# Output weights of two key heads in one transfer, mixed in pairs, in a decode attention kernel

## The chip, the cores and the metric

The kernel runs on one core of one Trainium2 chip. The metric is device time in microseconds (us) from launch to end, as the median of the executions in one set of rounds. Ratios below are the mean time of one kernel's fast runs over that of the kernel before's fast runs in the same rounds, so they are not quite the ratios of the medians quoted. A run counts as slow when it is over 1.5% above the fastest of its kernel; the medians and ranges below are of all runs, slow ones included. The profiled span is 1.7 to 3.1 us shorter than the time of the same execution. PE is TensorE, DVE is VectorE, ACT is ScalarE, SP is the engine that issues most DMAs. "Key tile 6" is the 4 MiB of keys of key head 6; heads are counted from 0.

## The reference, cut to what matters

```python
# B = 2, one query position, D = 448, 16 query heads on 8 key heads, Dh = 256, window W = 4096
q = (layernorm(x) @ wq)                       # 2 x 4096
p = softmax(q k^T / 16)                       # last 4096 cached keys of each key head
o = p v                                       # 2 x 16 x 256
out = x + o.reshape(2, 4096) @ wo + mish_mlp(layernorm(x))     # wo: 4096 x 448
```

The cached keys and values are 8 heads x (4 + 4) MiB. The output weights `wo` are 3.5 MiB, 512 rows of 896 bytes for each key head.

## The kernel before

Nearly everything streams through one DMA queue (77.66 of 77.81 MB), on which SP issues the loads. Per key head these are the next keys, the values, and the head's output weights:

```python
for i in range(Hkv + 1):
    if i + 1 < Hkv:
        load_k(i + 1, ...)
    if i < Hkv:
        load_v(i, ...)
        load_wo(i, parts=1 if i < Hkv - 1 else 2)
        for piece in range(NH):               # four pieces of a head's scores
            s = i * NH + piece
            if s + 1 < NSTEP: turn(s + 1)     # DVE transposes keys: kt <- k
            if piece == 1 and i > 1: finish(i - 2)
            scores(s)                         # PE: sc <- kt,qdiag, then exp on ACT
            ...
            if piece == 0 and i > 1: turn_o(i - 2)
            if piece == 1 and i > 1: mix(i - 2)
    ...
    if i >= 1: values(i - 1) or values_fixed(i - 1)   # the latter for heads 6 and 7
```

So the attention output of head i-2 is turned, scaled and multiplied with its weights ("mixed") inside head i. The heads 0 to 5 use this layout: partition p holds the four rows 4p to 4p+3 of the head's weights, one run of 3584 bytes, and mixing is four products over 128 partitions:

```python
wo_pool = tc.tile_pool(name="wo", bufs=3)
nc.sync.dma_start(out=w[:].rearrange("p h n -> p (h n)"),
    in_=A_wo[r0 : r0 + rep * Dh, :].rearrange("(p j) d -> p (j d)", p=P))   # load_wo
...
for j in range(NJ):                           # turn_o: NJ = 4, fp32, 8 rows x 128 columns
    for u in range(NP):                       # NP = 2
        nc.tensor.matmul(pqv[:, j, :], lhsT=o_sb[:, u, j, :, :]..., rhs=ident_f[...])
...
for j in range(NJ):                           # mix
    add(oT[:, j, :], w[...][:, j, :])         # psE += oT^T w, 2 x 448
```

In the trace of this kernel the 8 fp32 products of a turn leave 16 records a head (96 in the group of L516), the 4 bf16 products of a mix leave 4 (24 in that of L220).

After the last head, `mix(6)` (four products), a copy of the sum (`early`), `values_fixed(7)` and `mix(7)` follow one another on PE.

The softmax here doesn't subtract the row's maximum and nothing guards it: scores larger than these inputs give would overflow.

Of the kernel before, what the change touches and what calls it, by code (L numbers as in the profile page):

```python
# [9 lines left out]
ALU = mybir.AluOpType  # L10
AXIS = mybir.AxisListType
BF16 = mybir.dt.bfloat16
# [22 lines left out]
def kernel(  # L35
# [13 lines left out]
    nc = tc.nc  # L49
    P = 128  # L50
# [3 lines left out]
    Bsz, Sq, D = A_x.shape  # L54
    _, Hkv, Sk, Dh = A_k_cache.shape
    HqDh = A_wq.shape[1]
    Hq = HqDh // Dh
    rep = Hq // Hkv
    W = min(4096, max(256, Sk // 4))
    s0 = Sk - W  # L60
    F = B_w1.shape[1]
# [4 lines left out]
    BR = Bsz * rep  # L66
    NX = 2
    NS = D * NX // P
    HW = HqDh // NX
    HF = F // NX  # L70
    HH = Hq // NX
    NF = HF // P
    ND = Dh // P
# [8 lines left out]
    lead = ctx.enter_context(tc.tile_pool(name="lead", bufs=1))  # L82
    ident = lead.tile([P, P], BF16)
    hsel = lead.tile([P, Q], FP32)
    wo_pool = ctx.enter_context(tc.tile_pool(name="wo", bufs=3))
    k_pool = ctx.enter_context(tc.tile_pool(name="kk", bufs=2))
    v_pool = ctx.enter_context(tc.tile_pool(name="vv", bufs=2))
    kt_pool = ctx.enter_context(tc.tile_pool(name="kt", bufs=4))
    consts = ctx.enter_context(tc.tile_pool(name="consts", bufs=1))
    p_pool = ctx.enter_context(tc.tile_pool(name="pp", bufs=3))  # L90
    small = ctx.enter_context(tc.tile_pool(name="small", bufs=3))
# [6 lines left out]

    x_bf = consts.tile([Bsz, D], BF16)
    nc.scalar.dma_start(out=x_bf[:, :], in_=A_x.flatten_outer_dims())  # L100
    b1_sb = consts.tile([1, F], BF16)
    nc.scalar.dma_start(out=b1_sb[:, :], in_=B_b1.rearrange("(o f) -> o f", o=1))


    def v_tile():
# [7 lines left out]
    for lo, hi in ((0, SC), (SC, NS)):  # L113
# [16 lines left out]
        out=rstd[:], in_=mv[:, 1:2], func=ACT.Sqrt, bias=eps_t[:], scale=1.0  # L130
# [5 lines left out]
    for r in range(2):  # L136
        n = (NS + 1 - r) // 2
        nc.vector.tensor_scalar(  # L138
            out=xn_bf[:, r : NS : 2, :, :],
            in0=bass.AP(  # L140
                x_all.tensor,
                x_all.offset,
                [list(x_all.ap[0]), [1, n], [NS, P // 2], [(NS + r) // 2, 2]],
            ),
# [7 lines left out]
    for j in range(1, NQ):  # L152
        nc.vector.tensor_tensor(
            out=hsel, in0=hsel, in1=ident[:, j * Q : (j + 1) * Q : HS], op=ALU.add
# [4 lines left out]
    for b in range(Bsz):  # L159
        nc.vector.tensor_reduce(  # L160
            out=off[:, b : b + 1], in_=hsel[:, b * rep : (b + 1) * rep], axis=AXIS.X, op=ALU.add
# [4 lines left out]
        out=off[:], in0=off[:], scalar1=mine[:], scalar2=1e4, op0=ALU.subtract, op1=ALU.mult  # L166
    )

    PH = P // rep
    own = consts.tile([P, Bsz, rep], FP32)  # L170
    for h in range(rep):
        nc.vector.tensor_reduce(
            out=own[:, :, h],
            in_=ident[:, h * PH : (h + 1) * PH].unsqueeze(1).to_broadcast([P, Bsz, PH]),
            axis=AXIS.X,
            op=ALU.add,
        )
    ones_f = consts.tile([P, P], FP32)
# [10 lines left out]
    for s in range(NS):  # L189
# [7 lines left out]
        out=odd[:],  # L197
# [21 lines left out]
    def add(lhsT, w, start=False, stop=False):  # L219
        nc.tensor.matmul(  # L220
            psE[:], lhsT=lhsT, rhs=w, start=start, stop=stop, skip_group_check=True
        )
# [79 lines left out]
    def load_dense():  # L302
        w = v_tile()
        dense["w1"] = w[:, 0 : NS * HF].rearrange("p (s n) -> p s n", s=NS)
        nc.sync.dma_start(
            out=dense["w1"],
            in_=B_w1.rearrange("r (x n) -> (r x) n", x=NX).rearrange("(p s) n -> p s n", s=NS),
        )
        dense["w2"] = w[:, NS * HF : NS * HF + NX * NF * D].rearrange(
            "p (x c d) -> p x c d", x=NX, c=NF  # L310
        )
        nc.sync.dma_start(
            out=dense["w2"], in_=B_w2.rearrange("(x q c) d -> q x c d", x=NX, q=P)
        )

    def dense_in():
        w1_v = dense.pop("w1").rearrange("p s (q c) -> p s c q", c=NF)
        b1_v = b1_sb[:].rearrange("o (x q c) -> o x c q", x=NX, c=NF)
        hT_ps = ps_m.tile([P, NF, NX, Bsz], FP32, tag="m", name="hT_ps")
        for c in range(NF):  # L320
            for s in range(NS):
                nc.tensor.matmul(
                    hT_ps[:, c, :, :].rearrange("p x b -> p (x b)"),
                    lhsT=w1_v[:, s, c, :],
                    rhs=xs[:, s, :, :].rearrange("p x b -> p (x b)"),
                    start=(s == 0),
                    stop=False,
                    skip_group_check=True,
                )
            for x in range(NX):  # L330
                nc.tensor.matmul(
                    hT_ps[:, c, x, :],
                    lhsT=b1_v[:, x, c, :],
                    rhs=ones[:, :],
                    start=False,
                    stop=True,
                    skip_group_check=True,
                )
        shape = [P, NF, NX, Bsz]
        h_sb = consts.tile(shape, FP32, name="h_sb")  # L340
        nc.vector.tensor_copy(out=h_sb[:], in_=hT_ps[:])
        u_sb = consts.tile(shape, FP32, name="u_sb")
        nc.scalar.activation(out=u_sb[:], in_=h_sb[:], func=ACT.Exp)
        t_sb = consts.tile(shape, FP32, name="t_sb")
        nc.vector.scalar_tensor_tensor(
            out=t_sb[:], in0=u_sb[:], scalar=2.0, in1=u_sb[:], op0=ALU.add, op1=ALU.mult
        )
        den = consts.tile(shape, FP32, name="den_sb")
        nc.vector.tensor_scalar(
            out=den[:], in0=t_sb[:], scalar1=2.0, scalar2=None, op0=ALU.add  # L350
        )
        nc.vector.reciprocal(out=den[:], in_=den[:])
        nc.vector.tensor_tensor(out=t_sb[:], in0=t_sb[:], in1=den[:], op=ALU.mult)
        nc.vector.tensor_tensor(out=act_bf[:], in0=h_sb[:], in1=t_sb[:], op=ALU.mult)  # L354
# [27 lines left out]
        v_t[i] = t[:].rearrange("p (t d) -> p t d", t=T)  # L382

    def load_wo(kvh, parts=1):
        w = wo_pool.tile([P, rep, ND * D], BF16, tag="wo", name="wo")
        r0 = kvh * rep * Dh
        wo_t[kvh] = w
        if kvh < Hkv - NFIX:

            nc.sync.dma_start(  # L390
                out=w[:].rearrange("p h n -> p (h n)"),
                in_=A_wo[r0 : r0 + rep * Dh, :].rearrange("(p j) d -> p (j d)", p=P),
            )
            return
        win = A_wo[r0 : r0 + rep * Dh, :].rearrange("(h p c) d -> p h (c d)", h=rep, p=P)
        for u in range(parts):
            hs = slice(u * rep // parts, (u + 1) * rep // parts)
            nc.sync.dma_start(out=w[:, hs, :], in_=win[:, hs, :])  # L398
# [64 lines left out]
        return rec  # L463

    NJ = Dh // PH
    assert rep == 2 and NJ == rep * ND
    NP = 2
    NR = NP * BR

# [39 lines left out]
    def turn_o(i):  # L509

        o_sb = state.pop(("o", i))
        pq = ps_q.tile([P, NJ * BR], FP32, tag="q", name="q")
        pqv = pq[:].rearrange("p (j r) -> p j r", j=NJ)
        for j in range(NJ):
            for u in range(NP):
                nc.tensor.matmul(  # L516
                    pqv[:, j, :],
                    lhsT=o_sb[:, u, j, :, :].rearrange("r h m -> r (h m)"),
                    rhs=ident_f[0:NR, u * BR : (u + 1) * BR],
                    start=(u == 0 and j == 0),  # L520
                    stop=(u == NP - 1),
                    skip_group_check=True,
                )
        state["pq", i] = pqv

    def finish(i):
        pqv = state.pop(("pq", i))
        rec = state.pop(("rec", i))
        o = small.tile([P, NJ, Bsz, rep], FP32, tag="osum", name="osum")
        nc.vector.tensor_tensor(  # L530
            out=o[:].rearrange("p j b h -> p j (b h)"),
            in0=pqv,
            in1=rec[:].unsqueeze(1).to_broadcast([P, NJ, BR]),
            op=ALU.mult,
        )
        nc.vector.tensor_tensor(  # L536
            out=o[:].rearrange("p j b h -> p j (b h)"),
            in0=o[:].rearrange("p j b h -> p j (b h)"),
            in1=own[:].rearrange("p b h -> p (b h)").unsqueeze(1).to_broadcast([P, NJ, BR]),
            op=ALU.mult,  # L540
        )
        oT = small.tile([P, NJ, Bsz], BF16, tag="oTm", name="oTm")
        nc.vector.tensor_tensor(  # L543
            out=oT[:], in0=o[:, :, :, 0], in1=o[:, :, :, 1], op=ALU.add
        )
        state["oT", i] = oT

    def values_fixed(i):

# [16 lines left out]
        scale_o(i, po)  # L566

    def mix(kvh):
        oT = state.pop(("oT", kvh))
        w = wo_t.pop(kvh)  # L570
        put = add_last if kvh == Hkv - 1 else add
        if kvh < Hkv - NFIX:
            for j in range(NJ):
                add(oT[:, j, :], w[:].rearrange("p h (c d) -> p (h c) d", c=ND)[:, j, :])
            return
        for h in range(rep):
            for c in range(ND):
                put(
                    oT[:, c, h, :],
                    w[:, h, c * D : (c + 1) * D],  # L580
                    stop=(kvh >= Hkv - 2 and h == rep - 1 and c == ND - 1),
                )
# [80 lines left out]
```

## Time and profile before

| | before |
|---|---|
| median (first set of rounds) | 189.69 us, 6 runs, 189.51 to 193.02 (this last one slow) |
| profiled span | 187.9 us |
| DMA queue, share of 16 engines | 96.8% |
| PE, DVE, ACT busy | 81%, 57%, 24% |
| HBM read | 77.67 MB, 413 GB/s over the span |

The row to read first is the DMA share by slice: it is 8 or 9 tenths from the second slice to the last but one, so the bytes set the time as long as nothing behind the last byte is late. The lines of the page, the chain and the timeline that matter stand in the prediction.

### The profile page before, as it was taken

To read this page: it belongs to the slowest core of one execution; us is meant where nothing else is said; L and a number is where in the kernel's file an instruction comes from. 1 tells how busy PE (TensorE), PEld (TensorE's weight loads), DVE (VectorE), ACT (ScalarE), POOL (GpSimd) and SP (SyncE) were. 2 spreads that over 40 slices of the span, in tenths; PEclk is the share of its full clock that TensorE was granted. 3 is DMA by queue.
4 is the path that set the end of the run, shared out by engine and by line. 5 is a ranking of instruction groups with operands and counts; after the bars stand their busy time and mean duration, and the time that the engine had idled before them with its cause. 6 is when DMAs were issued, how large, how long until landed. Compare 5 with 4: busy or idle time off the path is not lost.

```text
span 187.9 us, 2493 instructions
## 1 busy us (share of the span) xinstructions
PE 151.5 (81%) x981; PEld 74.0 (39%) x981; DVE 106.9 (57%) x144; ACT 45.4 (24%) x148; POOL 16.5 (9%) x74
## 2 busy tenths in 40 slices
PE   0494099904989999979996999968995999999892
PEld 0141033901334364425342354434441534464781
DVE  5505497049671994089704991099506983976311
ACT  3005015200062225123322124033402223125101
POOL 7001500300003000200030003000110000000000
PEclk9999559965799999999999699999998799999955
DMA  6999899999999999999999999999999999999990
GB/s 224 420 474 446 376 434 439 439 443 446 433 446 419 406 407 436 446 439 393 472 445 440 412 426 412 440 446 418 451 433 439 394 436 419 443 439 415 412 381 27
DMA packets 5028, 77.81 MB, mean 414 GB/s; under 512 B 533, under 2 KB 1049, under 8 KB 2330
## 3 DMA queue, kind: packets, MB, share of 16 engines
q1 hardware_dynamic: 5012, 77.66, 96.8%
q8 instruction: 7, 0.11, 0.2%
q14 instruction: 3, 0.02, 0.0%
q10 hardware_dynamic: 6, 0.01, 0.0%
HBM read 77.67 MB, written 0.00 MB: 413 GB/s over the span
## 4 chain that ended last, share of the span: by engine, by line
DMA 67%; DVE 16%; PE 12%; SPq 2%; ACT 1%; issue 1%; ACTq 0%; DVEq 0%
DMA k<-in_A_k_cache_dram 57%; DVE kt L404 13%; DMA wo<-in_A_wo_dram 9%; PE sc L416 7%; PE o L477 4%; DVE pT L442 2%; SPq L373 1%; PE q L516 1%; ACT p L430 1%; PE psE L220 0%; SPq L114 0%; SPq L398 0%; PE psA L237 0%; DVE sums L451 0%; DVE osum L536 0%
## 5 line engine op out<-in xcount | busy, mean ns | idle before, releaser
L404 DVE STREAM_TRANSPOSE kt<-k 128x2048 f32<-128x2048 f32 x32 | 73.1, 2289 | 52.6 <-DMA k<-in_A_k_cache_dram 52.6
L416 PE MATMUL sc<-kt,qdiag 128*128 128x512 bf16 x256 | 65.2, 404 | 16.6 <-DVE kt L404 16.2
L430 ACT ACTIVATE p<-sc,off 128x256 bf16<-128x256 f32 x64 | 33.1, 544 | 70.9 <-PE sc L416 70.2
L416 PEld LDWEIGHTS <-qdiag 128*128 128x128 bf16 x256 | 23.8, 100 | 53.7 <-issue 23.5
L477 PE MATMUL o<-v,pT 128*8 128x512 bf16 x192 | 42.5, 379 | 0.0
L477 PEld LDWEIGHTS <-pT 128*8 128x8 bf16 x192 | 17.2, 92 | 22.4
L442 DVE STREAM_TRANSPOSE pT<-p 128x512 bf16<-128x512 bf16 x32 | 21.8, 681 | 5.8 <-ACT p L430 5.8
L289 POOL COPY qdiag<-qt 32x16 bf16<-32x16 bf16 x64 | 13.0, 249 | 120.0 <-PE sc L416 104.3
L486 ACT COPY o_sb<-o 8x512 f32<-8x512 f32 x12 | 6.3, 573 | 36.3 <-PE o L477 36.3
L516 PEld LDWEIGHTS q<-ident_f,o_sb 8*128 8x128 f32 x96 | 11.1, 186 | 3.1 <-issue 3.1
L430 ACT ACTIVATION_READ_ACCUMULATOR p<-sc,off 128x1 f32 x64 | 11.7, 183 | 0.0
L516 PE MATMUL q<-ident_f,o_sb 8*128 8x4 f32 x96 | 11.7, 249 | 0.0
L220 PE MATMUL psE<-v,act_bf 128*2 128x448 bf16 x14 | 4.9, 534 | 6.7 <-DVE act_bf L354 6.7
L269 PE MATMUL q_ps<-v,xq 128*128 128x512 bf16 x28 | 7.8, 446 | 2.5 <-DMA v<-in_A_wq_dram 2.5
L558 PEld LDWEIGHTS <-v 128*128 128x128 bf16 x256 | 7.4, 101 | 0.2 <-DMA v<-in_A_v_cache_dram 0.2
L558 PE MATMUL q<-pT,v 128*128 128x4 bf16 x256 | 7.4, 169 | 0.1
L220 PE MATMUL psE<-wo,oTm 128*2 128x448 bf16 x24 | 5.5, 352 | 1.4 <-DVE oTm L543 1.4
L269 PEld LDWEIGHTS <-xq 128*128 128x128 bf16 x28 | 3.1, 111 | 7.2 <-DVE xq L260 2.5
L279 DVE CAST q_sb<-q_ps 128x512 bf16<-128x512 f32 x2 | 1.3, 686 | 7.7 <-PE q_ps L269 7.7
L220 PEld LDWEIGHTS <-act_bf 128*2 128x2 bf16 x14 | 1.6, 117 | 9.7 <-DVE act_bf L354 6.8
L190 PE MATMUL xnT_ps<-ident,xn_bf 2*128 2x2 bf16 x7 | 0.5, 166 | 4.7 <-DVE xn_bf L138 4.7
L279 ACT CAST q_sb<-q_ps 128x512 bf16<-128x512 f32 x2 | 1.1, 589 | 12.0 <-PE q_ps L269 12.0
(62 smaller groups left out, 45.0 us busy)
## 6 DMA issues: line engine op xcount, KB each, us to landing
k<-in_A_k_cache_dram SPq DMA_DIRECT2D x7, 4096.0 KB, 27.3
v<-in_A_v_cache_dram SPq DMA_DIRECT2D x7, 4096.0 KB, 29.2
k<-in_A_k_cache_dram SPq DMA_DIRECT2D x2, 2048.0 KB, 24.6
v<-in_B_w_dram SPq DMA_DIRECT2D x2, 1568.0 KB, 24.5
wo<-in_A_wo_dram SPq DMA_DIRECT2D x7, 448.0 KB, 30.5
v<-in_A_wq_dram SPq DMA_DIRECT2D x1, 2048.0 KB, 7.4
v<-in_A_v_cache_dram SPq DMA_DIRECT2D x1, 2048.0 KB, 14.9
v<-in_A_wq_dram SPq DMA_DIRECT2D x1, 1536.0 KB
```

The lines of the kernel that those rows point to most:

```text
L220: nc.tensor.matmul(psE[:], lhsT=lhsT, rhs=w, start=start, stop=stop, skip_group_check=True)
L269: nc.tensor.matmul(ps[u][:], lhsT=xq[:, s, :, :].rearrange("p j k -> p (j k)"), rhs=wq_sb[:, s, u * N5 : (u + 1) * N5], start=(s == 0), st ...
L279: copy(out=q_sb[:, u * N5 : (u + 1) * N5], in_=ps[u][:])
L289: nc.gpsimd.tensor_copy(out=tv[rows, :, e, j * Q : (j + 1) * Q : HS].rearrange("p n (b h) -> p n b h", b=Bsz), in_=qv[rows, :, h0 : h0 + r ...
L404: nc.vector.transpose(out=kt[:].bitcast(FP32), in_=k[:, half * TH * Dh : (half + 1) * TH * Dh].bitcast(FP32),)
L416: nc.tensor.matmul(psc[:], lhsT=qdiag[i % NW][:, n * NE + e, :], rhs=ktv[:, n, e, :, :], start=(n == 0 and e == 0), stop=(n == NB - 1 and ...
L430: nc.scalar.activation(out=pv[:, b, :, :], in_=sv[:, b, :, :], func=ACT.Exp, scale=scale, bias=off[:, b : b + 1], accum_out=state["rs", i] ...
L442: nc.vector.transpose(out=pT[:], in_=p_t.pop(s)[:])
L477: nc.tensor.matmul(po[:], lhsT=pT_t[i * NH + piece][:, uh * NP * Q : (uh + 1) * NP * Q : HS], rhs=v[:, u * NP : (u + 1) * NP, :].rearrange ...
L486: nc.scalar.copy(out=o_sb[:, u, :, :, :], in_=po[:, u * Dh : (u + 1) * Dh] .rearrange("r (m j) -> r j m", j=NJ) .unsqueeze(2) .to_broadcas ...
L516: nc.tensor.matmul(pqv[:, j, :], lhsT=o_sb[:, u, j, :, :].rearrange("r h m -> r (h m)"), rhs=ident_f[0:NR, u * BR : (u + 1) * BR], start=( ...
L558: nc.tensor.matmul(po[:, c, :], lhsT=vv[:, t, c, :], rhs=pTv[:, th, 0:Q:HS], start=(t == 0 and c == 0), stop=(t == T - 1), skip_group_chec ...
```

## The change

The intent is longer runs and fewer transfers. Two key heads' weights (1024 rows) come in one transfer in which partition p holds eight rows, a run of 7168 bytes. The first head of a pair then lies on partitions 0 to 63 and the second on 64 to 127. The output of a head is turned with 64-column products onto its half of the partitions, and the pair is mixed together, eight products in the odd head. Two double buffers replace three single ones; the bias of the dense layer moves into the dense weights' tile to make room. Heads 6 and 7 keep their own layout.

```diff
-    wo_pool = ctx.enter_context(tc.tile_pool(name="wo", bufs=3))
+    wo_pool = ctx.enter_context(tc.tile_pool(name="wo", bufs=2))
...
-    PH = P // rep
+    NK = 2
+    PK = P // NK
+    PH = PK // rep
... (b1 load moved into the dense weights' tile; `own` mask rebuilt for two halves)
     def load_wo(kvh, parts=1):
+        if kvh < Hkv - NFIX:
+            if kvh % NK == 0:
+                w = wo_pool.tile([P, NJ * D], BF16, tag="wo", name="wo")
+                nc.sync.dma_start(
+                    out=w[:],
+                    in_=A_wo[r0 : r0 + NK * rep * Dh, :].rearrange("(p j) d -> p (j d)", p=P),
+                )
+                wo_t[kvh + NK - 1] = w
+            return
...
         pq = ps_q.tile([P, NJ * BR], FP32, tag="q", name="q")
+        k0 = i % NK * PK
+        pqv = pq[k0 : k0 + PK, :].rearrange("p (j r) -> p j r", j=NJ)
         for j in range(NJ):                      # NJ is now 8
             for u in range(NP):
                 nc.tensor.matmul(
...
+                    tile_position=(0, k0),
... (finish works on the head's half of the partitions)
     def mix(kvh):
+        if kvh not in wo_t:
+            return
...
-                add(oT[:, j, :], w[:].rearrange("p h (c d) -> p (h c) d", c=ND)[:, j, :])
+                add(oT[:, j, :], w[:, j * D : (j + 1) * D])
```

More of the change, by code (lines that the diff above doesn't have):

```diff
@@ L100 @@
     nc.scalar.dma_start(out=x_bf[:, :], in_=A_x.flatten_outer_dims())
-    b1_sb = consts.tile([1, F], BF16)
-    nc.scalar.dma_start(out=b1_sb[:, :], in_=B_b1.rearrange("(o f) -> o f", o=1))
     def v_tile():
@@ L173 @@
             out=own[:, :, h],
-            in_=ident[:, h * PH : (h + 1) * PH].unsqueeze(1).to_broadcast([P, Bsz, PH]),
-            axis=AXIS.X,
+            in_=ident[:].rearrange("p (k h m) -> p h k m", k=NK, h=rep)[:, h, :, :]
+            .unsqueeze(1)
+            .to_broadcast([P, Bsz, NK, PH]),
+            axis=AXIS.XY,
             op=ALU.add,
@@ L314, in load_dense @@
         )
+        lo = NS * HF + NX * NF * D
+        dense["b1"] = w[0:1, lo : lo + F]
+        nc.scalar.dma_start(out=dense["b1"], in_=B_b1.rearrange("(o f) -> o f", o=1))
     def dense_in():
         w1_v = dense.pop("w1").rearrange("p s (q c) -> p s c q", c=NF)
-        b1_v = b1_sb[:].rearrange("o (x q c) -> o x c q", x=NX, c=NF)
+        b1_v = dense.pop("b1").rearrange("o (x q c) -> o x c q", x=NX, c=NF)
         hT_ps = ps_m.tile([P, NF, NX, Bsz], FP32, tag="m", name="hT_ps")
@@ L384, in load_wo @@
     def load_wo(kvh, parts=1):
-        w = wo_pool.tile([P, rep, ND * D], BF16, tag="wo", name="wo")
         r0 = kvh * rep * Dh
-        wo_t[kvh] = w
-        if kvh < Hkv - NFIX:
-            nc.sync.dma_start(
-                out=w[:].rearrange("p h n -> p (h n)"),
-                in_=A_wo[r0 : r0 + rep * Dh, :].rearrange("(p j) d -> p (j d)", p=P),
-            )
-            return
+        if kvh < Hkv - NFIX:
[7 more added lines that the diff above has]
+            return
+        w = wo_pool.tile([P, NJ * D], BF16, tag="wo", name="wo")
+        w = w[:, 0 : rep * ND * D].rearrange("p (h n) -> p h n", h=rep)
+        wo_t[kvh] = w
         win = A_wo[r0 : r0 + rep * Dh, :].rearrange("(h p c) d -> p h (c d)", h=rep, p=P)
@@ L465 @@
     NJ = Dh // PH
-    assert rep == 2 and NJ == rep * ND
+    assert rep == 2 and (Hkv - NFIX) % NK == 0
     NP = 2
@@ L512, in turn_o @@
         pq = ps_q.tile([P, NJ * BR], FP32, tag="q", name="q")
-        pqv = pq[:].rearrange("p (j r) -> p j r", j=NJ)
+        k0 = i % NK * PK
+        pqv = pq[k0 : k0 + PK, :].rearrange("p (j r) -> p j r", j=NJ)
         for j in range(NJ):
@@ L528, in finish @@
         rec = state.pop(("rec", i))
+        rows = slice(i % NK * PK, (i % NK + 1) * PK)
         o = small.tile([P, NJ, Bsz, rep], FP32, tag="osum", name="osum")
+        ov = o[rows, :, :, :].rearrange("p j b h -> p j (b h)")
+        shape = [PK, NJ, BR]
         nc.vector.tensor_tensor(
-            out=o[:].rearrange("p j b h -> p j (b h)"),
-            in0=pqv,
-            in1=rec[:].unsqueeze(1).to_broadcast([P, NJ, BR]),
+            out=ov, in0=pqv, in1=rec[rows, :].unsqueeze(1).to_broadcast(shape), op=ALU.mult
+        )
+        nc.vector.tensor_tensor(
+            out=ov,
+            in0=ov,
+            in1=own[rows, :, :].rearrange("p b h -> p (b h)").unsqueeze(1).to_broadcast(shape),
             op=ALU.mult,
         )
+        if i % NK == 0:
+            state["oT", i + NK - 1] = small.tile([P, NJ, Bsz], BF16, tag="oTm", name="oTm")
         nc.vector.tensor_tensor(
-            out=o[:].rearrange("p j b h -> p j (b h)"),
-            in0=o[:].rearrange("p j b h -> p j (b h)"),
-            in1=own[:].rearrange("p b h -> p (b h)").unsqueeze(1).to_broadcast([P, NJ, BR]),
-            op=ALU.mult,
-        )
-        oT = small.tile([P, NJ, Bsz], BF16, tag="oTm", name="oTm")
-        nc.vector.tensor_tensor(
-            out=oT[:], in0=o[:, :, :, 0], in1=o[:, :, :, 1], op=ALU.add
-        )
-        state["oT", i] = oT
+            out=state["oT", i - i % NK + NK - 1][rows, :, :],
+            in0=o[rows, :, :, 0],
+            in1=o[rows, :, :, 1],
+            op=ALU.add,
+        )
     def values_fixed(i):
```

## The prediction

> **What bounds the kernel now.** I read the page first: the share of the DMA queues, then the row of slices.
>
> ```profile
> DMA  6999899999999999999999999999999999999990
> ...
> q1 hardware_dynamic: 5012, 77.66, 96.8%
> ```
>
> The one load queue keeps the 16 DMA engines busy for 96.8% of the span, and no slice but the first and the last is below 8 tenths. PE has 81% of the span busy and DVE 57%, so both should have spare time inside a head. Then the chain of waits in order of time, from the fifth key head on (start us, duration us, what):
>
> ```profile
> 112.92 29.40 DMA k<-in_A_k_cache_dram
> 142.31 0.02 issue
> 142.34 2.32 DVE kt L404
> 144.66 0.14 issue
> 144.80 3.44 PE sc L416 x8
> ...
> 156.51 7.02 PE o L477 x32
> ...
> 166.72 17.75 DMA wo<-in_A_wo_dram
> 184.47 0.04 issue
> 184.51 0.46 PE psA L237 x8
> ```
>
> It hops from one even key tile to the next (landings at 60.30, 101.30, 142.31, so 41.0 us for two heads), then goes through PE work, and ends in the landing of the last head's output weights. Two heads are 16 MiB of cache and 0.875 MiB of weights, 17.7 MB in 41.0 us or 431 GB/s: the stream sets the pace. What matters is whether the stream gets shorter, and whether anything at the tail stops fitting behind it. So third the timeline of PE at the end (start us, us, group, idle before it):
>
> ```profile
> 144.80 3.44 PE L416 MATMUL sc<-kt,qdiag 128*128 128x512 bf16 x8 [2.34 <-DVE kt L404]
> ...
> 165.30 1.94 PE L516 MATMUL q<-ident_f,o_sb 8*128 8x4 f32 x16
> 167.17 1.91 PE L416 MATMUL sc<-kt,qdiag 128*128 128x512 bf16 x8
> 169.02 0.92 PE L220 MATMUL psE<-wo,oTm 128*2 128x448 bf16 x4
> ...
> 179.87 3.96 PE L558 MATMUL q<-pT,v 128*128 128x4 bf16 x128
> 184.09 0.79 PE L237 MATMUL psA<-wo,oT 128*2 128x112 bf16 x16 [0.26 <-DVE oT L498]
> ```
>
> From the landing of key tile 6 PE works almost without a gap for 39 us, and it reaches the last output product at 184.09, only 0.4 us before the last weights land at 184.47. So there are two nearly equal paths to the end: the DMA stream, and "key tile 6 lands, then PE works through". Their margin is small: the wait for the last value piece (0.16 us in the timeline at 183.44) and the gap inside the last product (0.26 us at 184.52), together 0.42 us.
>
> [...]
> - [...] The trace agrees: in its packet records a 3584-byte packet takes 140 ns, 1792 bytes 74, 6272 bytes 239, 12544 bytes 469 and 32768 bytes 1213. The line through 1792 and 3584 leaves 8 ns at zero bytes; that through 6272 and 12544 leaves 9. At 3584 bytes the overhead is already only 6%.
> - [...] So bytes issued ahead of a key tile delay that key tile. The trace agrees as far as it goes: a 4 MiB load takes a median of 27 to 29 us from issue to landing, where its own bytes are worth 9.7 us at 431 GB/s; the rest is queue.
> - [...] The trace agrees for fp32: 128 columns take 187 ns (L516), 2 columns 76 ns (L237), so about 0.88 ns a column on a floor of 75.
> - [...] The clock row agrees (5s behind waits for keys):
>
> ```profile
> PEclk9999559965799999999999699999998799999955
> ```
>
> **The change part by part.**
>
> *Transfers.* Six weight loads of 128 packets of 3584 bytes become three of 128 packets of 7168. A 7168-byte packet should take 239 + 896 x 0.0367 = 272 ns (the slope from 6272 to 12544). Per engine, 6 x 8 x 140 = 6.72 us becomes 3 x 8 x 272 = 6.53 us, 0.19 us saved; three semaphore packets of 9 ns less give another 0.03. The stream gets about 0.2 us shorter, 0.1% of the span. That is all that longer runs can give.
>
> *Order of the loads.* This is the part that I think counts more. Both heads' weights now travel ahead of the next even key tile. Before key tile 6 the queue carried five weight tiles (5 x 8 x 140 = 5.60 us an engine); now three double ones (3 x 8 x 272 = 6.53). Key tile 6 lands 0.93 us later, less 0.02 for two semaphore packets: +0.9 us. Tiles 2 and 4 are some 1.0 us later in the same way; the odd ones and both halves of tile 7 are not.
>
> *Turning o.* One head used 8 products with 128 columns; it now uses 16 with 64, on half the partitions. fp32 runs twice, so 16 records become 32 (96 to 192 in all). Now 16 take 1.87 us in the chain, 117 ns each, against 28 ns for a bf16 weight load and product in L558 (128 in 3.55 us): so the fp32 weight load sets the pace. With 64 columns I expect a load record of 75 + 64 x 0.88 = 131 ns and a spacing of 117 - 56 = 61 ns, so 32 x 61 = 1.95 us a head, +0.1 us. Without a gain from the narrower load it would be 3.74 us, +1.9.
>
> *Mixing.* Four products of 0.22 us in each head (0.92 us by the timeline) become none in even heads and eight in odd ones. The sum stays; of the two heads behind key tile 6, the first loses 0.9 us and the second gets it. DVE's three small operations per head grow from 16 to 32 columns on 64 lanes, from 0.13 to some 0.15 us each, beside transposes of 2.3 us.
>
> *The buffer.* Two double weight buffers replace three single ones. The last head's weights now wait for mix(5), which ends at 169.9 and will end about 172, where their issue was at 166.1. But the queue still has about 10 us of values ahead of them then (head 7's values and weights are 4.4 MiB, 10.8 us, ending at 184.4), so the later issue is hidden. The earlier double tiles are freed a head before they are needed.
>
> *The bias.* Its 3.5 KB load moves behind the square root at about 3.9 us, into a tile not yet used; dense_in needs it some 25 us later. Nothing.
>
> *Sum.* DMA path: -0.2 us. PE path: +0.9 for key tile 6, +0.2 for two turns behind it, less the margin of 0.4: +0.7 us. The later path wins, so +0.7 if PE's clock behaves as before. It need not: behind key tiles 4 and 6 PE lost about 1.5 us to the halved clock (eight score products in 3.44 us against 1.91), after gaps of 2.32 and 2.34 us, while gaps of 1.31 and 1.63 us cost no half clock. The new gap ahead of tile 6 should be near 2.0 us, as PE reaches it later by tile 4's 1.0 us and two more turns, and the tile by 0.9. If it stays at full speed, PE has over 0.8 us in hand, and the DMA path ends the kernel 0.2 us sooner. I take a point between the two, 0.25 us above the median of 189.76: 190.0.
>
> **The rivals.**
> *Longer runs are worth much more.* It would need the weights to stall the engines beyond their packet times. Against it: the queue's packets fill 96.8% of the span, and the weights before are 6.7 us an engine in total; even if they came at the speed of the 32768-byte packets, 27.0 bytes a ns, they would take 6.37 us. Gain at most 0.4 us: 189.4.
> *The narrow fp32 products cost as much as wide ones.* Then PE gets 1.9 us per head. For it: I have no 64-column fp32 load in this trace. Two turns behind key tile 6 make 3.8 more, and the end comes about 4 us later: 194. Against it: the 2-column load, at 76 ns.
> *The late weights stall the tail.* If the wait for mix(5) reached past the queue's backlog, the DMA would run dry. About 10 us of backlog against 6 us of delay speak against it; if it failed by a microsecond or two, 191 to 192.
> *Nothing at all:* if the clock behaves, 189.5.
>
> **The range and the chances.** From 189.4 (gain of the stream alone) to 191.2 (+0.7 and a narrow product 20 ns slower than I think, 32 x 20 x 2 = 1.3 us, short of that in full). Faster by over 2% means under 186, for which no bytes or packets are there: 0.01. Slower by over 2% means over 193.6, which needs the second rival: 0.05. The rest, 0.94, is within 2%.
>
> **What would show it right or wrong.** The packet records should have 384 packets of 7168 bytes at about 272 ns. The chain should show even key tiles landing 0.7 to 1.0 us later (about 61.3, 102.3, 143.2). The group of L516, now 192 records, should have weight loads near 131 ns and a turn of about 2 us in the timeline. The last weights should be issued near 172 and still land by 184.5. The last product on PE should start between 184.0 and 184.9. I am wrong if a turn takes over 3 us, if the DMA share has a hole near the end, or if the last weights land after 185.

## The result, and the profile after

The changed kernel took 190.68 us (median of 6 runs, 190.21 to 191.49) against 189.69 for the kernel before. The ratio is 1.0061 with a 95% interval from 1.0033 to 1.0088: about 1.1 us slower, within 2%. A second set of rounds (`a0_again` below) gave 190.87 against 189.78, ratio 1.0050 (1.0037 to 1.0063).

The DMA queue after carries fewer packets and is a little less full (queue, kind: packets, MB, share of the 16 engines):

```profile
q1 hardware_dynamic: 4580, 77.66, 96.2%
```

The 5012 packets of before have become 4580: 384 packets fewer, and 48 fewer semaphore packets. The packet records show 384 packets of 7168 bytes with a median of 272 ns. The queue's share fell because the span grew: the packets took 181.9 us an engine in both, of 187.9 before and of 189.2 after.

The chain that ended last no longer ends in a DMA (start us, duration us, what):

```profile
114.67 28.56 DMA k<-in_A_k_cache_dram
143.24 0.02 issue
143.26 2.31 DVE kt L414
...
152.80 2.20 DVE kt L414
155.00 0.14 issue
155.14 1.90 PE sc L426 x8
...
169.81 1.60 PE psE L223 x8
...
178.79 1.67 PE psE L223 x4
...
185.89 0.65 PE psA L240 x14
```

Key tile 6 lands at 143.24 where it landed at 142.31. From there the chain stays on DVE for 12 us (four transposes of keys and what lies between them), then on PE to the end. The last weights landed at 184.51 by the trace, 1.4 us before PE used them.

The timeline of PE in the same stretch, the answer to the one in the prediction (start us, us, group, idle before it):

```profile
145.72 1.90 PE L426 MATMUL sc<-kt,qdiag 128*128 128x512 bf16 x8 [1.84 <-DVE kt L414]
...
151.83 1.90 PE L426 MATMUL sc<-kt,qdiag 128*128 128x512 bf16 x8 [0.42 <-DVE osum L545]
155.14 1.90 PE L426 MATMUL sc<-kt,qdiag 128*128 128x512 bf16 x8 [1.40 <-DVE kt L414]
156.87 0.28 PE L468 MATMUL den<-sums,ones_f 128*128 128x4 f32 x2
...
165.94 2.02 PE L527 MATMUL q<-ident_f,o_sb 8*64 8x4 f32 x32
...
169.74 1.68 PE L223 MATMUL psE<-wo,oTm 128*2 128x448 bf16 x8
...
174.84 0.28 PE L468 MATMUL den<-sums,ones_f 128*128 128x4 f32 x2
...
178.79 1.65 PE L223 MATMUL psE<-wo,oT 128*2 128x448 bf16 x4 [0.26 <-DVE oT L508]
...
182.07 3.56 PE L573 MATMUL q<-pT,v 128*128 128x4 bf16 x128
185.89 0.54 PE L240 MATMUL psA<-wo,oT 128*2 128x112 bf16 x16 [0.26 <-DVE oT L508]
```

For the same places, the end of head 6, the end of head 7 and `mix(6)`, the kernel before has these lines in its timeline:

```profile
156.24 0.28 PE L458 MATMUL den<-sums,ones_f 128*128 128x4 f32 x2
...
173.37 0.28 PE L458 MATMUL den<-sums,ones_f 128*128 128x4 f32 x2
...
177.31 0.92 PE L220 MATMUL psE<-wo,oT 128*2 128x448 bf16 x4 [0.26 <-DVE oT L498]
```

Four things are to be seen. Head 6 has no mix any more, and PE waits there for DVE instead: 0.42 and 1.40 us. Head 7 has eight products, 1.68 us instead of 0.92. A turn takes 2.02 us instead of 1.94. And `mix(6)`, the same four products in both kernels, takes 1.65 us instead of 0.92. The clock records of the trace say why: PE's clock fell to half at 177.2 us in this execution and at 178.7 in that of before, each time after the 128 products with four columns of `values_fixed(6)` had begun (after: while they ran; before: 1.6 us after their end and with `mix(6)` done).

PE's lateness against before adds up along the timeline. The end of head 6's scores (`den`) comes at 156.87 instead of 156.24: +0.63. The turn (+0.08) and the mix (+0.76) of head 7 bring `den` of head 7 to 174.84 instead of 173.37: +1.47. The slow `mix(6)` adds 0.73, so the last value products start at 182.07 instead of 179.87: +2.20. Before, these took 3.96 us with their wait for the last values, now 3.56: the last product starts 1.80 us later. As before it still waited a moment for the weights inside the last product, the final sums were read 1.57 us later (186.54 against 184.97 in the two chains), and the span grew by 1.3 us.

### The profile page after: what moved, and what is told of

It is laid out like the page before. It is cut to its first block, busy times and chain, and to the rows that moved or that the text cites. A ratio compares the mean times of both kernels' runs of the same rounds, so it can differ in the third digit from the quotient of the medians.

```text
span 189.2 us, 2687 instructions
## 1 busy us (share of the span) xinstructions
PE 152.6 (81%) x1077; PEld 76.2 (40%) x1077; DVE 108.1 (57%) x144; ACT 45.4 (24%) x148; POOL 16.4 (9%) x74
## 3 DMA queue, kind: packets, MB, share of 16 engines
q1 hardware_dynamic: 4580, 77.66, 96.2%
## 4 chain that ended last, share of the span: by engine, by line
DMA 57%; PE 21%; DVE 19%; ACT 1%; issue 1%; SPq 0%; ACTq 0%; DVEq 0%
DMA k<-in_A_k_cache_dram 57%; DVE kt L414 14%; PE sc L426 8%; PE o L487 4%; PE q L573 4%; PE q L527 3%; DVE pT L452 3%; PE psE L223 2%; PE psA L240 1%; ACT p L440 1%; SPq L112 0%; PE den L468 0%; DVE early L252 0%; DVE osum L548 0%; DVE oTm L556 0%
## 5 line engine op out<-in xcount | busy, mean ns | idle before, releaser
L426 PE MATMUL sc<-kt,qdiag 128*128 128x512 bf16 x256 | 64.2, 400 | 17.6 <-DVE kt L414 16.9
L527 PEld LDWEIGHTS q<-ident_f,o_sb 8*64 8x64 f32 x192 | 13.2, 147 | 3.0 <-issue 3.0
L527 PE MATMUL q<-ident_f,o_sb 8*64 8x4 f32 x192 | 13.7, 203 | 0.0
L272 PE MATMUL q_ps<-v,xq 128*128 128x512 bf16 x28 | 8.5, 479 | 3.0 <-DMA v<-in_A_wq_dram 3.0
L223 PE MATMUL psE<-v,act_bf 128*2 128x448 bf16 x14 | 4.2, 471 | 6.6 <-DVE act_bf L360 6.6
L223 PE MATMUL psE<-wo,oTm 128*2 128x448 bf16 x24 | 5.0, 352 | 0.8 <-DVE oTm L556 0.8
```

The costliest lines, as they stand in the source:

```text
L223: nc.tensor.matmul(psE[:], lhsT=lhsT, rhs=w, start=start, stop=stop, skip_group_check=True)
L272: nc.tensor.matmul(ps[u][:], lhsT=xq[:, s, :, :].rearrange("p j k -> p (j k)"), rhs=wq_sb[:, s, u * N5 : (u + 1) * N5], start=(s == 0), st ...
L426: nc.tensor.matmul(psc[:], lhsT=qdiag[i % NW][:, n * NE + e, :], rhs=ktv[:, n, e, :, :], start=(n == 0 and e == 0), stop=(n == NB - 1 and ...
L527: nc.tensor.matmul(pqv[:, j, :], lhsT=o_sb[:, u, j, :, :].rearrange("r h m -> r (h m)"), rhs=ident_f[0:NR, u * BR : (u + 1) * BR], start=( ...
```

## The experiments

The theory after reading the two traces: the kernel had two nearly equal paths to the end, the stream and PE behind key tile 6. The change delays key tile 6, and it takes PE work out of head 6, where PE then only waits for DVE, and puts it into head 7, where nothing waits. The rivals: (A) the last head's weights, now issued behind `mix(5)`, stall the end; (B) 32 narrow products cost more than 16 wide ones; (C) the place of the mixing is worth nothing, as the prediction had it.

### e1: the double loads behind the odd head

```diff
-            if kvh % NK == 0:
+            if kvh % NK == NK - 1:
+                r0 -= (NK - 1) * rep * Dh
...
-                wo_t[kvh + NK - 1] = w
+                wo_t[kvh] = w
```

> The changed kernel with each double weight load issued after the values of the odd head of its pair instead of the even one, so only two of them (not three) stand ahead of key tile 6. My theory (the end sits on PE behind the landing of key tile 6 and the doubled mix in head 7): key tile 6 lands near 141.1 us (142.3 before, 143.2 in the changed kernel), the wait of PE for it is gone, the end falls back on the last weights, ratio to before 0.998 to 1.002. Rival A (the last head's weights are issued late, behind mix(5), and stall the end): that wait is still here, 1.006 as changed. Rival B (32 narrow fp32 products cost PE more than 16 wide ones): still here, 1.006.

Measured: 190.50 us (189.73 to 192.04, 6 runs) against 190.11, ratio 1.0036 (0.9995 to 1.0077). Key tile 6 landed by 141.07, as expected, but the gain is not clear. Two of the six runs were at 189.73 and 189.76, as the theory has it; others reached 191.7 and 192.0. In the profiled run the wait of PE had moved to key tile 5 (3.16 us before its first scores at 124.21), and PE's clock was at half for 10.2 us behind it; eight mix products took 2.73 us there. From that key tile on the chain had no DMA in it. So the edit moved the wait by one head rather than removing it, and the experiment does not decide by itself.

### e2, e3 and e4: the order of the loads and the place of the mixing, apart and together

These three start from the kernel before with four single weight buffers and the bias moved, so runs of 3584 bytes, wide turns, and no late weights.

```diff
 # e2 (and e4): both heads' loads at the even head
-            load_wo(i, parts=1 if i < Hkv - 1 else 2)
+            if i >= Hkv - NFIX:
+                load_wo(i, parts=1 if i < Hkv - 1 else 2)
+            elif i % 2 == 0:
+                load_wo(i)
+                load_wo(i + 1)
 # e3 (and e4): the even head's mix next to the odd head's
     def mix(kvh):
+        if kvh < Hkv - NFIX:
+            if kvh % 2 == 0:
+                return
+            mix_one(kvh - 1)
+        mix_one(kvh)
```

> The kernel before with single weight tiles, but both heads' loads issued at the even head (four single buffers instead of three, and the bias moved as in the change to make room). Nothing else of the change. My theory: key tile 6 lands about 1.1 us later than before (143.4), PE reaches the last product 0.4 to 1.1 us later, ratio 1.002 to 1.006. Rivals A and B: neither the late issue nor the narrow products are in it, 1.000.

> The kernel before with the loads in their old places, but the four products of an even head's mix moved to the odd head, next to the other four (same four buffers and bias as in e2_order_only). My theory: key tile 6 lands as before at 142.3; in head 6 PE gains little, as it then waits for DVE's turned keys; in head 7 it has 0.75 us more to do; PE reaches the last product 0.1 to 0.9 us later, ratio 1.001 to 1.005. Rival (the sum of the products is the same, so their place is worth nothing, as my prediction had it): 1.000.

> e2_order_only and e3_mix_only together: the change without its long runs, narrow products and late weights. My theory: the whole of the loss, ratio 1.005 to 1.009, a little over the changed kernel's since short runs add 0.2 us ahead of key tile 6. If the narrow products or the late weights are part of the loss, less than that, 1.000 to 1.004.

| kernel | median us | before, same rounds | ratio (95%) | key tile 6 by | `den` of head 6 | `den` of head 7 | last product starts |
|---|---|---|---|---|---|---|---|
| before (its profile) | | | | 142.3 | 156.24 | 173.37 | 184.09 |
| e2, order only | 189.76 | 190.11 | 0.9997 (0.9968 to 1.0025) | 143.3 | 156.78 | 173.92 | 184.23 |
| e3, mix only | 190.14 | 190.11 | 1.0007 (0.9993 to 1.0021) | 142.2 | 155.69 | 173.57 | 184.62 |
| e4, both | 191.63 | 190.11 | 1.0063 (1.0036 to 1.009) | 143.3 | 156.76 | 174.65 | 185.70 |
| changed kernel (its profile) | | | | 143.2 | 156.87 | 174.84 | 185.89 |

(One run of e2, one of e4 and two of the kernel before were slow; the ratios leave them out.)

e4 reproduces the whole loss, without long runs, narrow products or late weights. Each half alone costs nothing that these rounds can see. That is less than I expected of e2, and of e3 too, though both intervals still hold the lower edge of what I expected. The timelines say how the two fit together. First e2 (mix in both heads), then e4 (none in head 6, eight products in head 7):

```profile
152.14 0.92 PE L218 MATMUL psE<-wo,oTm 128*2 128x448 bf16 x4 [0.72 <-DVE oTm L544]
152.99 3.96 PE L417 MATMUL sc<-kt,qdiag 128*128 128x512 bf16 x16
156.78 0.28 PE L459 MATMUL den<-sums,ones_f 128*128 128x4 f32 x2
...
169.57 0.92 PE L218 MATMUL psE<-wo,oTm 128*2 128x448 bf16 x4
```

```profile
155.02 1.90 PE L417 MATMUL sc<-kt,qdiag 128*128 128x512 bf16 x8 [1.39 <-DVE kt L405]
156.76 0.28 PE L459 MATMUL den<-sums,ones_f 128*128 128x4 f32 x2
...
169.54 1.67 PE L218 MATMUL psE<-wo,oTm 128*2 128x448 bf16 x8
```

With key tile 6 at the same time, head 6 ends at 156.78 with four mix products in it and at 156.76 with none: taking them out gains 0.02 us, because the last scores wait for DVE's fourth transpose. In head 7 the four more cost 0.73 us (173.92 to 174.65). That refutes rival C for a head 6 in which the clock stays full. At half clock I have only two different kernels to compare: `den` of head 6 came 13.93 us after the landing of key tile 6 before, with four mix products, and 13.64 us after it in `a0_look1` below, with none. So there too the removal was worth some 0.3 us and not 0.92.

e2 brings the last value products 0.54 us later than before (180.41 against 179.87), and the last product only 0.14 us; its last weights landed at 184.41, when it had already begun, and the final sums were read at 184.92, no later than before (184.97). The margin took up the delay. e3 loses 0.20 us by `den` of head 7, which the margin would take up too. Its last product starts 0.53 us later: the 0.20, 0.73 more for a `mix(6)` at half clock (1.65 us), less 0.40 for the wait for the last values that fell away. Only the two together are clearly past the margin.

### a0_again, e5 and e6: the changed kernel, with short runs, and with the last weights early

```diff
 # e5: the double load in two halves of 3584-byte runs
-                nc.sync.dma_start(out=w[:], in_=A_wo[...].rearrange("(p j) d -> p (j d)", p=P))
+                win = A_wo[...].rearrange("(p j) d -> p (j d)", p=P)
+                hw = NJ * D // 2
+                for u in range(2):
+                    cols = slice(u * hw, (u + 1) * hw)
+                    nc.sync.dma_start(out=w[:, cols], in_=win[:, cols])
 # e6: heads 6 and 7 share one double buffer
-        w = wo_pool.tile([P, NJ * D], BF16, tag="wo", name="wo")
-        w = w[:, 0 : rep * ND * D].rearrange(...)
+        if kvh == Hkv - NFIX:
+            state["w_fix"] = wo_pool.tile([P, NJ * D], BF16, tag="wo", name="wo")
+        lo = (kvh - (Hkv - NFIX)) * rep * ND * D
+        w = state["w_fix"][:, lo : lo + rep * ND * D].rearrange(...)
```

A first form of e6, with a separate tile for the last weights, did not build for want of 3.5 KB a partition and never ran; the record holds no trace of it.

> The changed kernel again, unaltered, beside the others on one chip. Theory: 1.004 to 1.009. The e-runs so far show that the end is PE's and that the four products of mix(6) take 0.9 us at full clock and 1.65 at half; where the clock falls differs from run to run. So I expect single runs to spread over 0.7 us or more (before: half of that, as its end has a margin behind the weights). If the spread is no larger than before's, the clock is not the reason.

> The changed kernel with each double weight load cut in two loads of 3584-byte runs, same bytes in the same places. My theory: the packets go back from 384 of 272 ns to 768 of 140, the stream is 0.2 us longer and key tile 6 lands 0.15 us later; ratio to before 0.000 to 0.002 above that of a0_again. Rival (longer runs are worth much more): 0.005 or more above it.

> The changed kernel with the last head's weights in the free half of the buffer of head 6, so that they no longer wait for mix(5). My theory: they are issued near 166.5 instead of 171.4 and land at the same 184.5, as the queue is full until then; the ratio is that of a0_again within 0.002. Rival A (the late issue costs the end): back to 1.000 to 1.002.

| kernel | median us | before, same rounds | ratio (95%) |
|---|---|---|---|
| a0_again | 190.87 | 189.78 | 1.0050 (1.0037 to 1.0063) |
| e5, short runs (two of 6 slow) | 191.31 | 189.78 | 1.0059 (1.0042 to 1.0077) |
| e6, early weights | 190.62 | 189.78 | 1.0049 (1.0027 to 1.0070) |

Short runs are 0.0009 above the changed kernel, with intervals that overlap. That excludes the 0.005 of the rival that longer runs are worth much more; a difference as small as the 0.2 us that the packets save these runs cannot tell from none. (The profile of e5 fell in a slow run and is used for its packets alone: 768 of 3584 bytes at a median of 140 ns, besides the bias.) With early weights the ratio is the same. They were issued at 166.9 instead of 171.3 and landed at 184.4 instead of 184.3. Rival A is out.

Rival B is out by e4, which has the whole loss with wide products, and by the groups of the two pages (line, engine, op, shapes | busy us, mean ns | idle before), before and after:

```profile
L516 PEld LDWEIGHTS q<-ident_f,o_sb 8*128 8x128 f32 x96 | 11.1, 186 | 3.1 <-issue 3.1
```

```profile
L527 PEld LDWEIGHTS q<-ident_f,o_sb 8*64 8x64 f32 x192 | 13.2, 147 | 3.0 <-issue 3.0
```

The median of the narrow load is 133 ns (the mean of 147 has 32 loads at half clock in it, with a median of 222). By columns the fp32 loads of the two traces take 76 ns for 2, 133 for 64 and 187 for 128.

### e8: the kernel before with the weights one head later

e1 to e4 point to a version of the kernel before that gives PE more margin: let each head's weights stand behind one more key tile.

```diff
+            if i >= 1:
+                load_wo(i - 1)
             load_v(i, ...)
-            load_wo(i, parts=1 if i < Hkv - 1 else 2)
+            if i == Hkv - 1:
+                load_wo(i, parts=2)
```

> The kernel before with one edit: each head's weights are loaded one head later, just ahead of the next head's values, so that four instead of five weight tiles stand ahead of key tile 6 (five instead of six ahead of tile 7). My theory: key tile 6 lands 1.1 us earlier, near 141.2, PE gets that much margin at the end, and the end stays with the last weights: ratio 0.997 to 1.000, with a narrower spread than before. If the key's landing has nothing to do with the end, 1.000 and the same spread; if loading weights later makes mix wait, over 1.002.

Measured: 189.67 us (189.59 to 190.05, 5 runs) against 189.78 (189.60 to 190.02, 11 runs), ratio 0.9992 (0.9979 to 1.0004). Key tile 6 landed by 141.15. In its profile `mix(6)` fell into the half clock (1.57 us), and yet the last product started at 184.13 and its weights landed at 184.57: PE had its margin, and the stream ended the kernel. The ratio is where the theory put it, but the interval holds 1; the spread is no narrower. Nothing was found that clearly beats the kernel before.

### e9 and the three looks: the place of the mixing again, and the clock

e9 is e4 with the grouped mixes in the even heads.

```diff
-            if kvh % 2 == 0:
+            if kvh % 2 == 1:
                 return
-            mix_one(kvh - 1)
+            if kvh > 0:
+                mix_one(kvh - 1)
```

(The group ends at head 4; head 5 is mixed alone.)

> e4_order_and_mix with the grouped mixes in the even heads instead of the odd ones: heads 4 and 6 have eight products, head 7 the four of mix(5) alone. Same loads in the same order, same sum of products. Theory (in head 6 PE waits 1.4 us for DVE's last turned keys, so products there are free; in head 7 nothing waits and each 0.2 us counts): key tile 6 lands at 143.3 as in e4, the last value products of head 5 begin within 0.5 us of e4's 156.97, mix in head 7 takes 0.9 us instead of 1.67, and the ratio falls from e4's 1.006 to 1.000 to 1.003. Rival (doubled mixing costs wherever it stands, or the late key tile alone makes the loss): 1.005 or more.

Measured: 191.05 us (189.84 to 191.46, 6 runs) against 190.02, ratio 1.0049 (1.0022 to 1.0075). This expectation failed. Head 7 did lose its extra products, 0.92 us instead of 1.67, but head 6 was not free:

```profile
145.75 3.36 PE L417 MATMUL sc<-kt,qdiag 128*128 128x512 bf16 x8 [3.28 <-DVE kt L405]
...
152.76 1.67 PE L218 MATMUL psE<-wo,oTm 128*2 128x448 bf16 x8
...
157.87 0.28 PE L459 MATMUL den<-sums,ones_f 128*128 128x4 f32 x2
```

In this run the clock fell to half at key tile 6: eight score products took 3.36 us instead of 1.90. Head 6 has about 1.8 us of waiting to fill (1.40 and 0.42 in the changed kernel). The half clock needs 1.46 of it and the eight products 1.67, together 3.1, and `den` came 1.1 us later than in e4. Head 5 no longer mixes, so PE came early, and its wait ahead of key tile 6 grew from 1.82 us in e4, where the clock stayed full, to 3.28. That the longer wait brought the half clock about is my guess from one profile of each. The measured ratio is that of the rival. Its second form, the late key tile alone, is out by e2; its first, that doubled mixing beside a late key tile costs in either head, is not. One run of e9, at 189.84, was as fast as the kernel before; whether its clock had stayed full I cannot say, as only one run of each kernel has a trace.

The three looks ask how much of the spread of the changed kernel is the clock.

> The changed kernel once more for its profile: where mix(6) (the four products that follow the first half of the last head's work) takes 1.65 us, the halved clock having begun before it, the span should be near 189.0, and where it takes 0.92, near 188.4, as in the three profiles so far (189.2 and 189.0 with 1.65, 188.4 with 0.92, the last with the weights' own buffer). If the spans do not follow this, the clock is not what spreads the times.

> As a0_look1, a second profile: a span near 189.0 with mix(6) at 1.65 us, near 188.4 with 0.92.

> As a0_look1, a third profile: a span near 189.0 with mix(6) at 1.65 us, near 188.4 with 0.92.

| profile | half clock from | `mix(6)` starts | `mix(6)` takes | last product starts | span |
|---|---|---|---|---|---|
| changed, first | 177.2 | 178.79 | 1.65 | 185.89 | 189.2 |
| a0_again | 178.3 | 178.66 | 1.65 | 185.75 | 189.0 |
| a0_look2 | 179.2 | 178.89 | 1.34 | 185.67 | 189.0 |
| a0_look1 | 179.4 | 178.88 | 1.13 | 185.56 | 188.9 |
| e6 | 180.0 | 178.79 | 0.92 | 185.15 | 188.4 |
| a0_look3 | 180.4 | 178.90 | 0.92 | 185.26 | 188.6 |

The three looks are single runs, 191.07, 191.22 and 190.39 us, so their state is unknown; their spans follow the table. The later the half clock begins, the shorter `mix(6)` and, by and large, the span; `mix(6)` starts within 0.25 us in all six. So in these profiles most of the spread of 0.8 us is where the clock falls. With `mix(6)` at full clock (e6 and a0_look3) the last product still starts 1.06 and 1.17 us later than before (184.09): the half clock is not the whole loss. In a0_again the five runs spread over 0.73 us and the eleven of before over 0.42, as expected, as far as so few runs can tell.

## Why the prediction was right or wrong

The range and the class held: 190.0 was forecast with 189.4 to 191.2, and 190.68 and 190.87 were measured. The gain that one might expect of longer runs went as the prediction said it would: there was hardly any. That the range held was partly luck. Its upper end had room for narrow products 20 ns slower than expected, and these came as expected (61 ns each); the room was filled by costs that the sum did not have. Without it the PE path gave at most 0.7 us above 189.76, or 190.5. One of the prediction's own signs failed as well: the last product should have started between 184.0 and 184.9, and it started between 185.26 and 185.89 in the five profiles of the changed kernel.

- *Transfers, -0.2 us of stream.* Right for the packets: 272 ns each, 384 of them. That the stream ends 0.2 us sooner was not seen: the last weights landed between 184.30 and 184.57 us in the five profiles of the changed kernel, and between 184.41 and 184.57 in the six of kernels with short runs (before, e2, e3, e4, e8, e9). In the total it cannot show, since the stream no longer ends the kernel.
- *Order of the loads, key tile 6 +0.9 us.* Right: 142.31 became 143.24. e2 shows that this alone stays within the margin of the end.
- *Turning o, +0.1 us a head.* Right: 131 ns expected and 133 measured for the load, 1.95 us expected and measured in the chain. The rival of +1.9 us a head is gone.
- *The buffer, nothing.* Right: issued at 171.4, landed at 184.51, and e6 without the wait is no faster.
- *Mixing, "the sum stays; the first loses 0.9 us and the second gets it".* This step failed. It treated two heads of PE work as one account. The 0.9 us taken out of head 6 turned into a wait for DVE (e2 and e4: 0.02 us gained), and the 0.75 us put into head 7 counted in full. This term of the sum should have been +0.75, not 0.
- *The clock at key tile 6.* The prediction hoped that a full clock there would leave PE over 0.8 us in hand. The clock did stay full in the first profile after a gap of 1.84 us (1.90 us for eight score products), and nothing was left over: DVE's fourth transpose ended 11.6 to 11.8 us after the landing in the six profiles read for it (before, first after, e4, e9, looks 1 and 3), with PE at half clock there or at full. In the three looks the clock was at half there and `den` of head 6 came at 156.96 to 156.98, against 156.87 and 156.75 at full clock. The four gaps of before (2.32 and 2.34 us with half clock behind them, 1.31 and 1.63 with full) did not carry over: eight score products took 1.90 us behind 2.60 us in a0_again and behind 2.24 in e3, and 3.16 behind 2.02 in a0_look3. So the length of the gap alone did not tell, and what decides was not shown.
- *The clock at the end.* `mix(6)` at half clock, 0.73 us, was not in the sum. It is the largest single part of the difference between the profiles of the changed kernel. In the first profile after, the clock fell at 177.2 us while `values_fixed(6)` ran without a gap (128 products with four columns each in 3.55 us, from 174.98). Why it fell there was not shown.

The predicted +0.7 for an unchanged clock came from +0.9 and +0.2 less 0.4 of margin. The first profile shows, at the last value products, +0.63 by the end of head 6, +0.84 in head 7 and +0.73 at `mix(6)`. That the first of these is below 0.9 is because before, head 6 had both its mix and the half clock (1.54 us) to bear, while after it runs on DVE's pace. What is left open is how much of the unprofiled difference of about 1 us is the clock: the trace of one run in each set is all there is.

## What to carry to other kernels

Where a stream and an engine end within half a microsecond of each other, ask of every edit on which side of the last wait it puts the work: here work removed ahead of a wait for another engine was worth 0.02 us, and the same work added behind it counted in full (0.73 us). Nor is such a wait safely free room: e9 filled about 1.8 us of it with 1.67 us of products, and a fall of the clock took 1.46 us too. A small margin can hide each of two edits and not their sum, so test them apart and together. Before coalescing transfers, read the fixed cost from the packet records (here 272 ns for 7168 bytes against 280 for twice 3584), and count the bytes that the larger transfer puts ahead of the next one that somebody waits for (here 0.9 us for key tile 6).
